# Decode attention with a gated FFN: K and V in pairs of heads, wo as the last load

## The chip, the cores and the metric

The kernel runs on one NeuronCore of a Trainium2 chip. The metric is device time in microseconds (us), the median of several executions. Times come from runs in the fast state. A profile shows one execution: its "span" is 1.5 to 1.8 us shorter than the measured time of the same execution, so spans are compared with spans.

## The reference

Two sequences, one query token each, 32 heads of 128, a cache of 4096 keys. In short:

```python
q = (x @ wq) per head                      # wq 512 x 4096
p = softmax(q k^T / sqrt(128))             # k_cache, v_cache: 2 x 32 x 4096 x 128, bf16
a = concat_heads(p v) @ wo                 # wo 4096 x 512
b = relu(x @ w1) @ w2                      # FFN, 1376 wide
g = sigmoid(sum(x * gate_w))
out = g * a + (1 - g) * b
```

K and V are 134 MB of the 145.4 MB that must come from HBM. Everything else is small.

## The kernel before

One load is one head of K or V, 1 MB, one row of 8 KB in each of 128 partitions, into one of 8 slots. All K heads come first, then all V heads. w1 and w2 are loaded after the sixth K head, wo in the middle of K.

```python
    for n in range(128):
        s = n % NSLOT                                   # NSLOT = 8
        waits = []
        if n >= NSLOT:
            prev = n - NSLOT
            waits.append(f"T_{prev}_3" if prev < 64 else f"pv_{prev - 64}")
        P.add("sp", lambda e, n=n, s=s: e.dma_start(kv_sb[:, s, :], kv_in(n)), ...)
        # [...] w1, w2 at n == 5, wo at n == 40
```

So a K slot is free when its transposes are done, a V slot when its product with p (PV) is done. For each K head TensorE (PE) makes 32 transposes (T) into PSUM; VectorE (DVE) and ScalarE (ACT) copy them to SBUF; then 8 score matmuls (Sc) follow. Each goes to one of four column groups of the array, given by `tile_position`. PE runs one head ahead: T of head i+1 stands before Sc of head i.

```python
    def S_chunk(g, c):
        p0 = 32 * (c % 4)                               # column group
        return bank(2 * g + c // 4, 0, 512, p0, p0 + 32)
    # [...]
    for g in range(2):                                  # batch
        P.begin_loop(NIT)
        for p in range(PER):
            T((p + 1) % PER, lambda t, g=g, p=p: 32 * g + PER * t + p + 1)
            Sc(g, p)                                    # c = 0..7, 512 columns each
        P.end_loop()
    # [...]
    ptrans(0)                                           # p of batch 0 to PV's layout
    denom(0)
    # [...] PV of batch 0
    ptrans(1)
    denom(1)
    # [...]
    ffn_h()                                             # FFN, between the two halves of V
    ffn_f()
    # [...] PV of batch 1, projection of each head after it
```

Of the kernel before, what the change touches and what calls it, by code (L numbers as in the profile page):

```python
# [13 lines left out]
NSLOT = 8  # L14
PER = 8
NIT = 32 // PER
# [3 lines left out]
class _Op:  # L20
    __slots__ = ("fn", "waits", "signal", "sem")

    def __init__(self, fn, waits, signal, sem):
        self.fn = fn
        self.waits = waits
        self.signal = signal
        self.sem = sem

# [8 lines left out]
class _Prog:  # L37
# [19 lines left out]
    def add(self, engine, fn, waits=(), signal=None, sem=None):  # L57
        op = _Op(fn, waits, signal, sem or engine + "_ev")
        if engine == "pe" and self.loop is not None:
            self.loop.ops.append(op)  # L60
        else:
            self.streams[engine].append(op)
# [8 lines left out]
    def _count(self, op, name, counts, inc):  # L71
        if name is None:
            return
        counts[op.sem] = counts.get(op.sem, 0) + inc
        assert name not in self.marks, name
        self.marks[name] = (op.sem, counts[op.sem])

    def resolve(self):
        counts = {}
        for e in self.ENGINES:  # L80
            for it in self.streams[e]:
                if isinstance(it, _Loop):
                    for t in range(it.n):
                        for op in it.ops:
                            if op.signal is not None:
                                self._count(op, op.signal(t), counts, 1)
                else:
                    self._count(it, it.signal, counts, 16 if e == "sp" else 1)
# [22 lines left out]
    def emit(self, engine, eng):  # L111
        for it in self.streams[engine]:
            if isinstance(it, _Loop):
                lin = [self._linear(op, it.n) for op in it.ops]
                with eng.Fori(0, it.n) as iv:
# [5 lines left out]
                    for op, ws in zip(it.ops, lin):  # L121
# [3 lines left out]
                        if op.signal is not None:  # L125
                            ins.then_inc(self.sem(op.sem), 1)
            else:
# [3 lines left out]
                if it.signal is not None:  # L131
                    ins.then_inc(self.sem(it.sem), 16 if engine == "sp" else 1)


def bass_gated_mix__gqa_block_cached__dense_activation_relu__decode_kernel(
# [17 lines left out]
    jmask = sb("jmask", [128, 32], f32)  # L153
    ones = sb("ones", [128, 128], f32)
# [13 lines left out]
    kv_sb = sb("kv_sb", [128, NSLOT, 4096], b16)  # L168
    kt_sb = sb("kt_sb", [128, NKT, 32, 128], b16)
    qmask = sb("qmask", [128, 64, 32], b16)  # L170
    qst = sb("qst", [128, PER, 32], b16)
    E_sb = [sb(f"E{g}", [128, 1024], b16) for g in range(2)]
    pst = sb("pst", [128, PER, 32], b16)
# [8 lines left out]
    oT = sb("oT", [128, 32, 2], b16)  # L182
# [18 lines left out]
    PT_BANK = (0, 2)  # L201
    MISC = 1
    A_BANK = 3
    HT0 = 0

    def o_col(p):
        return bank(4 + p % 4, p, 1)
# [3 lines left out]
    w1_in = B_w1.rearrange("(t p) f -> p t f", p=128)  # L211
    w2a_in = B_w2[0:1280, :].rearrange("(t p) n -> p t n", p=128)
    w2b_in = B_w2[1280:1376, :]
    wq_in = A_wq.rearrange("(t p) n -> p t n", p=128)
    wo_in = A_wo.rearrange("(h d) n -> d h n", d=128)
    out_ap = out.rearrange("b s d -> (b s) d")

    def kv_in(n):
        c = A_k_cache if n < 64 else A_v_cache
        b, h = divmod(n % 64, 32)  # L220
        return c[b, h].rearrange("(p r) d -> p (r d)", p=128)


    def load(name, dst, src, waits=()):
        P.add("sp", lambda e: e.dma_start(dst, src), waits=waits, signal=name, sem=name)  # L225

    load("ld_x", x_sb[:, :], x_in)
    load("ld_gw", gw_sb[:, :], gw_in)
    load("ld_wq", wq_sb[:, :, :], wq_in)
    for n in range(128):  # L230
        s = n % NSLOT
        waits = []
        if n >= NSLOT:
            prev = n - NSLOT
            waits.append(f"T_{prev}_3" if prev < 64 else f"pv_{prev - 64}")
        P.add("sp", lambda e, n=n, s=s: e.dma_start(kv_sb[:, s, :], kv_in(n)),  # L236
              waits=waits, signal=f"ld_kv_{n}", sem=f"slot{s}")
        if n == 5:
# [3 lines left out]
        if n == 40:  # L242
            load("ld_wo", wo_sb[:, :, :], wo_in)
    P.add("sp", lambda e: e.dma_start(out_ap, out_sb[:, :]), waits=["res"], signal="st", sem="st")
# [14 lines left out]
    P.add("pool", lambda e: e.memset(ones[:], 1.0), signal="c_one")  # L259
    P.add("dve", lambda e: e.memset(zt[:], 0.0), signal="c_zt")  # L260
# [7 lines left out]
    for t in range(4):  # L268
        P.add("pe", lambda e, t=t: e.transpose(bank16(4, 2 * t, 2), x_sb[0:2, t * 128:(t + 1) * 128], ident16[0:2, 0:2]),
              waits=["c_id", "ld_x"] if t == 0 else [], signal="xT" if t == 3 else None)  # L270
    for t in range(4):
        P.add("pe", lambda e, t=t: e.transpose(bank16(5, 2 * t, 1), gw_sb[0:1, t * 128:(t + 1) * 128], ident16[0:1, 0:1]),
# [25 lines left out]
    def evac_eng(p, q):  # L298
        return "act" if q == 3 or (q == 1 and p % 2) else "dve"

    def T(p, head, only=None):

        for q in range(4):
            for rr in range(8):
                r = 8 * q + rr

                def waits(t, q=q):
                    i = head(t)
                    return ([f"ld_kv_{i}"] if q == 0 else []) + ([f"ev_{i - 1}_{q}"] if i else [f"qm_{g}" for g in range(2)] + ["g"])

                def sig(t, q=q):
                    return f"T_{head(t)}_{q}"

                def fn(e, *_, q=q, rr=rr, r=r):
                    return e.transpose(bank16(4 + q, rr * 128, 128), kv_sb[:, p, r * 128:(r + 1) * 128], ident16[:, :])  # L315
                w = (waits if P.loop else waits(0)) if rr == 0 else []
                s = (sig if P.loop else sig(0)) if rr == 7 else None
                P.add("pe", fn, waits=w, signal=s)

    def Sc(g, p):  # L320
        for c in range(8):
            def fn(e, *_, c=c):
                return e.matmul(S_chunk(g, c), lhsT=qst[:, p, :], rhs=kt_sb[:, p % NKT, 4 * c:4 * c + 4, :],  # L323
                                start=False, stop=True, tile_position=(0, 32 * (c % 4)), skip_group_check=True)

            def waits(t):
                i = 32 * g + PER * t + p
                return [f"qst_{i}"] + [f"ev_{i}_{q}" for q in range(4)]
            P.add("pe", fn, waits=waits if c == 0 else [], signal=(lambda t: f"sc_{32 * g + PER * t + p}") if c == 7 else None)

    def evac(i):
        p = i % PER
        for q in range(4):
            src = bank16(4 + q, 0, 1024).rearrange("p (r c) -> p r c", r=8)
            dst = kt_sb[:, i % NKT, 8 * q:8 * q + 8, :]
            w = [f"T_{i}_{q}"] + ([f"sc_{i - NKT}"] if i >= NKT else [])
            if evac_eng(p, q) == "dve":
                P.add("dve", lambda e, dst=dst, src=src: e.tensor_copy(out=dst, in_=src), waits=w, signal=f"ev_{i}_{q}", sem=f"ev{p}{q}")  # L338
            else:
                P.add("act", lambda e, dst=dst, src=src: e.activation(out=dst, in_=src, func=ACT.Copy), waits=w,  # L340
                      signal=f"ev_{i}_{q}", sem=f"ev{p}{q}")

    def stage_q(i):
        p = i % PER
        P.add("pool", lambda e: e.tensor_copy(out=qst[:, p, :], in_=qmask[:, i, :]),  # L345
              waits=[f"qm_{i // 32}"] + ([f"sc_{i - PER}"] if i >= PER else []), signal=f"qst_{i}", sem=f"qs{p}")

    T(0, lambda t: 0)
    for g in range(2):
        P.begin_loop(NIT)  # L350
        for p in range(PER):
            T((p + 1) % PER, lambda t, g=g, p=p: 32 * g + PER * t + p + 1)
# [4 lines left out]
    def row_max(g):  # L357
        P.add("dve", lambda e: e.tensor_reduce(out=m4[:, g:g + 1], in_=S_region(g), axis=AX.X, op=ALU.max),  # L358
              waits=[f"sc_{32 * g + 31}"], signal=f"m4_{g}")
# [15 lines left out]
    def ptrans(g):  # L375
        for cc in range(4):
            for k in range(8):
                c = cc if k < 4 else cc + 4
                r = 4 * c + k % 4
                col0 = (c // 4) * 512 + (k % 4) * 128  # L380
                pq = 32 * cc
                P.add("pe", lambda e, r=r, pq=pq, col0=col0: e.transpose(  # L382
                    bank16(PT_BANK[g], r * 32, 32), E_sb[g][pq:pq + 32, col0:col0 + 128], ident16[pq:pq + 32, pq:pq + 32],
                    tile_position=(pq, 0)),
                    waits=[] if k else [f"pt_{g}_{cc - 1}" if cc else f"E_{g}"], signal=f"pt_{g}_{cc}" if k == 7 else None)

    def denom(g):
        P.add("dve", lambda e: e.tensor_scalar(out=lm[:, g, :], in0=jmask[:, :], scalar1=l4[:, g:g + 1], scalar2=None, op0=ALU.mult),
              waits=[f"E_{g}", "c_j4"], signal=f"lm_{g}")
        P.add("pe", lambda e: e.matmul(bank(MISC, 32 * g, 32), lhsT=ones[:, :], rhs=lm[:, g, :], start=True, stop=True),  # L390
              waits=[f"lm_{g}", "c_one"] + (["rg_0"] if g else []), signal=f"lb_{g}")
# [5 lines left out]
    def stage_p(i):  # L397
        g, j = divmod(i, 32)
        p = i % PER
        P.add("dve", lambda e: e.tensor_copy(out=pst[:, p, :], in_=PSB[:, 1024 * PT_BANK[g] + j:1024 * PT_BANK[g] + 1024:32]),  # L400
              waits=[f"pt_{g}_3"] + ([f"pv_{i - PER}"] if i >= PER else []), signal=f"pst_{i}", sem=f"ps{p}")

    def o_norm(i):
        g, j = divmod(i, 32)
        p = i % PER
        P.add("dve", lambda e: e.tensor_scalar(out=oT[:, j, g:g + 1], in0=o_col(p), scalar1=rg[:, g, j:j + 1], scalar2=None, op0=ALU.mult),  # L406
              waits=[f"pv_{i}", f"rg_{g}"], signal=f"oT_{i}", sem=f"on{p}")

    def PV(g, p):
        for r in range(32):  # L410
            def waits(t):
                i = 32 * g + PER * t + p
                return [f"ld_kv_{64 + i}", f"pst_{i}"] + ([f"oT_{i - 4}"] if i >= 4 else [])
            P.add("pe", lambda e, iv, r=r: e.matmul(o_col(p), lhsT=kv_sb[:, p, r * 128:(r + 1) * 128], rhs=pst[:, p, r:r + 1],  # L414
                                                    start=(r == 0), stop=(r == 31)),
# [125 lines left out]
```

## Time and profile before

| | before |
|---|---|
| time, median | 356.31 us |
| span of the profile (that execution took 356.67 us) | 354.9 us |
| bytes moved | 145.4 MB, 427 GB/s for most of the span |
| last packet of the loads | 350.0 us |

The page of a profile cuts the span into 40 slices: a digit is an engine's busy share in tenths, PEclk is the granted TensorE clock, GB/s what the DMA engines moved. The chain of waits is followed back from the last instruction to what released each step. The lines are shown in the prediction. The main reading: DMA bounds the whole, PE bounds nothing but is full during K.

### The profile page before, as it was taken

To read this page: it belongs to the slowest core of one execution; us is meant where nothing else is said; L and a number is where in the kernel's file an instruction comes from. 1 tells how busy PE (TensorE), PEld (TensorE's weight loads), DVE (VectorE), ACT (ScalarE), POOL (GpSimd) and SP (SyncE) were. 2 spreads that over 40 slices of the span, in tenths; PEclk is the share of its full clock that TensorE was granted. 3 is DMA by queue.
4 is the path that set the end of the run, shared out by engine and by line. 5 is a ranking of instruction groups with operands and counts; after the bars stand their busy time and mean duration, and the time that the engine had idled before them with its cause. 6 is when DMAs were issued, how large, how long until landed. Compare 5 with 4: busy or idle time off the path is not lost.

```text
span 354.9 us, 11090 instructions
## 1 busy us (share of the span) xinstructions
PE 259.1 (73%) x4951; PEld 201.4 (57%) x4951; DVE 134.3 (38%) x323; ACT 100.3 (28%) x105; POOL 16.6 (5%) x77
## 2 busy tenths in 40 slices
PE   2498499999999844999999773344345995665655
PEld 1386387777877733778777573334344563443432
DVE  1056266766666831666676521111100221111101
ACT  1036066556566561556655300000000000000000
POOL 3010000000000000000000000000000000000000
PEclk9999699999999995999999955555555565555555
DMA  7999999999999999999999999999999999999992
GB/s 278 428 423 386 410 424 428 425 428 427 428 427 429 404 352 424 428 428 428 428 428 428 425 420 425 428 428 427 428 428 428 427 422 428 428 425 428 427 426 90
DMA packets 25036, 145.68 MB, mean 411 GB/s; under 512 B 2133, under 2 KB 7610, under 8 KB 8122
## 3 DMA queue, kind: packets, MB, share of 16 engines
q1 hardware_dynamic: 25018, 145.44, 98.6%
q8 instruction: 12, 0.20, 0.2%
q14 instruction: 6, 0.05, 0.0%
HBM read 145.43 MB, written 0.00 MB: 410 GB/s over the span
## 4 chain that ended last, share of the span: by engine, by line
DMA 52%; PE 38%; SPq 8%; issue 1%; DVE 0%
DMA kv_sb<-in_A_v_cache_dram 41%; PE PS L315 28%; DMA kv_sb<-in_A_k_cache_dram 11%; PE PS L323 8%; SPq L225 8%; PE PS L414 2%; SPq L236 1%; PE PS L421 0%; DVE out_sb L490 0%; PE PS L382 0%
## 5 line engine op out<-in xcount | busy, mean ns | idle before, releaser
L315 PEld LDWEIGHTS PS<-ident,kv_sb 128*128 128x128 bf16 x2080 | 121.9, 100 | 44.5 <-issue 32.9
L315 PE MATMUL PS<-ident,kv_sb 128*128 128x128 bf16 x2080 | 132.9, 224 | 17.1 <-DMA kv_sb<-in_A_k_cache_dram 15.5
L338 DVE COPY kt_sb<-PS 128x1024 bf16<-128x1024 bf16 x160 | 104.9, 687 | 70.6 <-PE PS L315 70.5
L340 ACT ACTIVATE kt_sb<-PS 128x1024 bf16<-128x1024 bf16 x96 | 94.9, 1022 | 94.9 <-PE PS L315 94.9
L414 PE MATMUL PS<-pst,kv_sb 128*128 128x1 bf16 x2048 | 62.8, 165 | 62.4 <-DMA kv_sb<-in_A_v_cache_dram 60.5
L414 PEld LDWEIGHTS PS<-pst,kv_sb 128*128 128x128 bf16 x2048 | 59.2, 104 | 77.5 <-issue 70.9
L406 DVE TENSOR_SCALAR oT<-PS,rg 128x1 bf16<-128x1 f32 x64 | 14.1, 221 | 125.4 <-PE PS L414 125.4
L323 PE MATMUL PS<-kt_sb,qst 128*32 128x512 bf16 x512 | 39.8, 388 | 0.0
L433 ACT ACTIVATE hr_sb<-PS 128x20 f32<-128x20 f32 x1 | 0.2, 188 | 73.8 <-PE PS L429 73.8
L345 POOL COPY qst<-qmask 128x32 bf16<-128x32 bf16 x64 | 13.1, 211 | 161.7 <-PE PS L323 148.7
L421 PE MATMUL PS<-wo_sb,oT 128*2 x32 | 18.4, 574 | 0.0
L323 PEld LDWEIGHTS PS<-kt_sb,qst 128*32 128x32 bf16 x512 | 7.7, 94 | 6.7 <-issue 0.2
L288 PE MATMUL PS<-xT_sb,wq_sb 128*128 128x2 bf16 x128 | 3.6, 165 | 9.5 <-DMA wq_sb<-in_A_wq_dram 9.5
L400 DVE COPY pst<-PS 128x32 bf16<-128x32 bf16 x64 | 10.4, 180 | 0.0
L288 PEld LDWEIGHTS PS<-xT_sb,wq_sb 128*128 128x128 bf16 x128 | 3.5, 104 | 9.6 <-DMA wq_sb<-in_A_wq_dram 9.6
L444 PE MATMUL PS<-w_sb,hT_sb 128*2 128x512 bf16 (+1 forms) x11 | 4.9, 630 | 0.6 <-DVE hT_sb L436 0.6
L293 DVE TENSOR_SCALAR qmask<-PS 128x32 bf16<-128x32 f32 x2 | 0.4, 311 | 12.7 <-PE PS L288 12.7
L421 PEld LDWEIGHTS PS<-wo_sb,oT 128*2 x32 | 2.5, 79 | 2.4 <-issue 1.9
L371 ACT ACTIVATE E<-PS,negM 128x1024 bf16<-128x1024 f32 x2 | 2.2, 1114 | 4.7 <-DVE negM L366 4.7
L358 DVE TENSOR_REDUCE m<-PS 128x1 f32<-128x1024 f32 x2 | 2.4, 1219 | 2.8 <-PE PS L323 2.8
L382 PE MATMUL PS<-ident,E 32*128 32x32 bf16 x64 | 3.0, 179 | 0.4
L444 PEld LDWEIGHTS PS<-w_sb,hT_sb 128*2 128x2 bf16 (+1 forms) x11 | 1.2, 120 | 3.4 <-issue 2.7
(40 smaller groups left out, 24.6 us busy)
## 6 DMA issues: line engine op xcount, KB each, us to landing
kv_sb<-in_A_k_cache_dram SPq DMA_DIRECT2D x64, 1024.0 KB, 16.0
kv_sb<-in_A_v_cache_dram SPq DMA_DIRECT2D x64, 1024.0 KB, 18.5
wq_sb<-in_A_wq_dram SPq DMA_DIRECT2D x1, 4096.0 KB, 12.5
wo_sb<-in_A_wo_dram SPq DMA_DIRECT2D x1, 4096.0 KB, 27.8
w_sb<-in_B_w_dram SPq DMA_DIRECT2D x1, 1376.0 KB, 28.6
w_sb<-in_B_w_dram SPq DMA_DIRECT2D x1, 1280.0 KB, 30.9
w_sb<-in_B_w_dram SPq DMA_DIRECT2D x1, 96.0 KB, 22.3
x_sb<-in_A_x_dram SPq DMA_DIRECT2D x1, 2.0 KB
```

Of the source, the lines that this page charges most:

```text
L225: P.add("sp", lambda e: e.dma_start(dst, src), waits=waits, signal=name, sem=name)
L288: P.add("pe", lambda e, h=h, t=t: e.matmul(bank(7, 2 * h, 2), lhsT=wq_sb[:, t, h * 128:(h + 1) * 128], rhs=xT_sb[:, t, :], start=(t == 0), ...
L315: return e.transpose(bank16(4 + q, rr * 128, 128), kv_sb[:, p, r * 128:(r + 1) * 128], ident16[:, :])
L323: return e.matmul(S_chunk(g, c), lhsT=qst[:, p, :], rhs=kt_sb[:, p % NKT, 4 * c:4 * c + 4, :], start=False, stop=True, tile_position=(0, 3 ...
L338: P.add("dve", lambda e, dst=dst, src=src: e.tensor_copy(out=dst, in_=src), waits=w, signal=f"ev_{i}_{q}", sem=f"ev{p}{q}")
L340: P.add("act", lambda e, dst=dst, src=src: e.activation(out=dst, in_=src, func=ACT.Copy), waits=w, signal=f"ev_{i}_{q}", sem=f"ev{p}{q}")
L345: P.add("pool", lambda e: e.tensor_copy(out=qst[:, p, :], in_=qmask[:, i, :]), waits=[f"qm_{i // 32}"] + ([f"sc_{i - PER}"] if i >= PER el ...
L400: P.add("dve", lambda e: e.tensor_copy(out=pst[:, p, :], in_=PSB[:, 1024 * PT_BANK[g] + j:1024 * PT_BANK[g] + 1024:32]), waits=[f"pt_{g}_3 ...
L406: P.add("dve", lambda e: e.tensor_scalar(out=oT[:, j, g:g + 1], in0=o_col(p), scalar1=rg[:, g, j:j + 1], scalar2=None, op0=ALU.mult), wait ...
L414: P.add("pe", lambda e, iv, r=r: e.matmul(o_col(p), lhsT=kv_sb[:, p, r * 128:(r + 1) * 128], rhs=pst[:, p, r:r + 1], start=(r == 0), stop= ...
L421: return e.matmul(bank(A_BANK, 0, 512, 0, 2), lhsT=oT[:, bass.ds(h, 1), :], rhs=wo_sb[:, bass.ds(h, 1), :], start=False, stop=True, skip_g ...
L444: P.add("pe", lambda e, ft=ft, n=n: e.matmul(bank(A_BANK, 0, 512, 0, 2), lhsT=hT_sb[0:n, ft, :], rhs=w2_sb[0:n, ft, :], start=(ft == 0), s ...
```

## The change

Its intent is fewer, longer DMA packets (16 KB rows), and a shorter end: wo arrives last, in pieces, and each piece is projected as it lands, so that attention's last steps are hidden behind wo. Heads come in pairs, 2 MB each, into 4 slots; head h of the pair lies in partitions 64h to 64h+63. PE no longer runs ahead; the scores of the two heads stand next to each other; FFN stands between K and V. The core of the diff:

```diff
-NSLOT = 8
-PER = 8
+NSLOT = 4
+PER = 4
+NPAIR = 16
[...]
     def kv_in(n):
-        c = A_k_cache if n < 64 else A_v_cache
-        b, h = divmod(n % 64, 32)
-        return c[b, h].rearrange("(p r) d -> p (r d)", p=128)
+        c = A_k_cache if n < 32 else A_v_cache
+        b, hp = divmod(n % 32, 16)
+        return c[b, 2 * hp:2 * hp + 2].rearrange("h (p r) d -> (h p) r d", p=64)
[...]
-        if n == 40:
-            load("ld_wo", wo_sb[:, :, :], wo_in)
+    WO_CUTS = (0, 16, 24, 28, 30, 32)
+    for k in range(5):
+        lo, hi = WO_CUTS[k], WO_CUTS[k + 1]
+        load(f"ld_wo_{k}", wo_sb[:, lo:hi, :], wo_in[:, lo:hi, :])
[...]
     def Sc(g, p):
         for c in range(8):
+            for hh in range(2):
[...]
+                P.add("pe", lambda e, iv, c=c, hh=hh: e.matmul(
+                    S_chunk(g, c), lhsT=qst[:, p, hh, :], rhs=kt_sb[:, p % NKT, 8 * c:8 * c + 8, 64 * hh:64 * hh + 64],
[...]
-    T(0, lambda t: 0)
     for g in range(2):
         P.begin_loop(NIT)
         for p in range(PER):
-            T((p + 1) % PER, lambda t, g=g, p=p: 32 * g + PER * t + p + 1)
+            T(g, p)
             Sc(g, p)
[...]
     ptrans(0)
     denom(0)
+    ffn_h()
+    ffn_relu()
+    ffn_f()
+    denom_l(1)
+    ptrans(1)
+    denom(1)
[...] PV of all pairs, then the projection, 64 matmuls of 256 columns
```

## The prediction

> **What bounds the kernel now.** First I read the page's slices and queue lines:
>
> ```profile
> PE   2498499999999844999999773344345995665655
> PEclk9999699999999995999999955555555565555555
> GB/s 278 428 423 386 410 424 428 425 428 427 428 427 429 404 352 424 428 428 428 428 428 428 425 420 425 428 428 427 428 428 428 427 422 428 428 425 428 427 426 90
> DMA packets 25036, 145.68 MB, mean 411 GB/s; under 512 B 2133, under 2 KB 7610, under 8 KB 8122
> ```
>
> A slice is 354.9/40 = 8.87 us. Transfers run at 427 GB/s from the second slice to the last but one, so 145.4 MB need 340.6 us; the other 14 us are the start, two dips (slices 3 to 5: w1/w2; 14 and 15: wo) and the end. DMA bounds the whole. The chain of waits says how far off the next bound is. The whole, by engine:
>
> ```profile
> DMA 52%; PE 38%; SPq 8%; issue 1%; DVE 0%
> ```
>
> The piece (start us, length us):
>
> ```profile
> 102.52 0.55 PE PS L323 x8
> 103.07 1.89 PE PS L315 x32
> 104.96 0.55 PE PS L323 x8
> 105.51 1.89 PE PS L315 x32
> ```
>
> During K the chain runs through PE. A head costs 32 transposes, 1.89 us, and 8 score matmuls, 0.55 us: 2.44 us. Its 1.049 MB cost 2.46 us at 427 GB/s. So PE and DMA are balanced to 1%, and PE has nothing to give away. The stretches confirm it: columns are busy us (instructions) of PE, PEld, DVE, ACT, POOL, then clock, DMA share, GB/s.
>
> ```profile
> 36.00:110.00 74.00, 69.49 (x1118) 55.02 (x1120) 45.83 (x70) 40.54 (x42) 5.71 (x27) 0.95 1.01 426
> 204.00:350.00 146.00, 84.21 (x2110) 64.14 (x2106) 20.22 (x124) 0.24 (x2) 0.00 (x0) 0.51 1.00 420
> ```
>
> K: PE full and DMA full. V: DMA full, PE half busy at half clock. Last, one head's scores, asked of the timeline twice, with a window that touches only the first four matmuls and one that touches all eight:
>
> ```profile
> 61.00 0.40 PE L323 MATMUL PS<-kt_sb,qst 128*32 128x512 bf16 x4
> ...
> 61.00 0.62 PE L323 MATMUL PS<-kt_sb,qst 128*32 128x512 bf16 x8
> ```
>
> Four end together after 0.40 us, eight after 0.62: two rounds 0.22 us apart. In the trace's start times the first four lie 3 ns apart, the next four begin 217 ns later, and the next transpose 0.55 us after the first. Chunks c=0..3 go to four column groups (32*(c%4)) and run side by side; c=4..7 wait for their groups.
>
> **What the Trainium skill says.** "TensorE: Matmul & The Clock Gate", Part 3, The mechanism: matmuls start and end in program order, with no reordering, though different tiles of the array overlap. The trace agrees as far as it shows (3 ns inside a round, 217 ns between rounds), but it has no matmul that follows another in the same group. Same page, Part 1: the array runs at half rate until a free-running window of 3.4 us was busy. Here the first transposes come 107 ns apart from 18.1 to 23.3 us, then 56; after the last scores the clock falls at 204.2 us, 5.45 us later. "DMA: Bandwidth & Descriptors", Why small descriptors are slow: a fixed cost per packet. The trace agrees: packets take 309 ns (8192 B), 109 (2752 B), about 48 (1024 B), which fits 8 ns plus bytes/27.2 per ns.
>
> **The change, part by part.**
>
> *Packets.* Rows of 16 KB, if they stay one packet, take 8 + 602 = 610 ns instead of 2 x 309. A pair (128 rows, 16 engines) takes 4.88 us; all of K and V save 64 x 0.064 = 4 us. wo took 4096 x 48/16 = 12.3 us, now 9.8; w1/w2 took 7.6, now 6.6. DMA's need falls by 7.5 us to about 339. This is the intended gain.
>
> *K on PE, the part that decides.* Sixteen score matmuls per pair, the same 512 in all, but in the order c0h0, c0h1, c1h0, c1h1: two heads of a chunk follow each other in one column group. c0h1 must wait for c0h0's 217 ns; c1h0 starts with c0h1; c1h1 waits again. Rounds: c0h0 | c0h1,c1h0 | c1h1,c2h0 | ... | c7h1, nine, instead of four. So 9 x 0.217 + 0.11 (drain: 0.55 - 2 x 0.217) = 2.06 us where two heads took 1.10. Transposes: 64 at 55.7 ns + 0.11 = 3.67 us. Also the eighth group of transposes waits for ACT's second copy (ACT does copies 1, 3, 5 at 1.02 us each; PE gets there at 3.12 us, ACT at about 3.24): 0.1. A pair is 5.8 us, against 4.88 for its DMA. PE becomes the bound of K. The later score waits (copies 4 to 7) are hidden by the slower scores.
>
> K starts when q is there. wq is now issued first on its queue, 0.7 us earlier: transposes from 17.4 us instead of 18.1. They are cold about 5.2 us, which loses 2.4. K ends at E = 17.4 + 2.4 + 32 x 5.8 = 205.4, say 205.5; before it ended at 198.75. PE does not wait for data: pair n starts at 19.8 + 5.8n, its data lands at about 17 + 4.9n (+6.6 after n=12). With four slots DMA is ahead and idles from pair 20 or so.
>
> *From K to V.* Before, DMA lagged behind PE: at 198.75 us 81.8 MB had moved, 3.6 of them V, four to five more heads lay queued, and the first PV (203.2) freed a slot before they ran out. Now DMA has nothing left: V0 to V3 fill the four slots, the last issued when pair 31's transposes end (E-2.06), landed at about E+4. V4 waits for the first PV, and all softmax and now also all FFN stand before it:
>
> ```profile
> 198.88 1.22 DVE L358 TENSOR_REDUCE m<-PS 128x1 f32<-128x1024 f32 x1 [2.75 <-PE PS L323]
> ...
> 201.61 1.11 ACT L371 ACTIVATE E<-PS,negM 128x1024 bf16<-128x1024 f32 x1 [4.68 <-DVE negM L366]
> ...
> 277.21 4.85 PE L444 MATMUL PS<-w_sb,hT_sb 128*2 128x512 bf16 x11 [0.61 <-DVE hT_sb L436]
> ```
>
> Maximum done E+2.8, exponentials E+4.1; rg_0 E+3.5 (reciprocal 0.36, scale 0.24); 44 FFN matmuls at 27 ns, E+4.8; relu and scaling, E+5.8; FFN's second layer 22 of 256 columns, cold half of the 427 ns start to start seen here, 4.7 us, E+10.5; transposes of p, 64 at 27 ns, E+12.2; denominator E+12.9; its reciprocal and staging E+13.9; PV of 64 at 26.5 ns and its signal E+15.8; V4's first packet 1.1 us after its issue (first wq packet 2.51 after issue at 1.42): about E+17, or E+14.5 if the clock is still warm. I take E+16: 12 us of idle DMA.
>
> *V and wo.* 28 pairs x 4.88 + wo 9.8 = 146.4 us of DMA. Data end D = 205.5 + 16 + 146.4 = 367.9; before 350.0.
>
> *The tail.* Before: last V landed 350.35, PV 1.0, projection 1.1, copy 0.68, store; span ends at 354.9, 4.9 us after the last packet. Now PV and spreading of o hide under wo. But 64 projection matmuls of 256 columns start only when half of wo is there, at D-4.5, and PE is cold: 213 ns each. If the clock rises about 5 us later (24 done), the other 40 take 109 ns: 9.5 us in all, done at D+5. Then copy about 0.4, store and end as before 1.9: D+7.3. The tail grows by about 2.4, though it was meant to shrink.
>
> Sum: 367.9 + 7.3 = 375 span, plus 1.4 (356.3 measured less 354.9 span) = 376.6. I say 376.
>
> **Rivals.** (a) The array runs c1h0 before c0h1, or the two heads side by side. Then scores take four rounds, but the pair still waits for the last PSUM copy: transposes end 3.67, DVE copies 6 and 7 at 0.69 each end near 4.85, scores 0.25 more: 5.15. E = 185, first PV E+16, DMA idle about 8 us: D near 348, end 355, reported 356. For it: different groups do overlap. Against it: the two heads of a chunk use the same group, and order is kept by the page. (b) DMA bound all through, as intended: D = 340.4, plus 3 us of gap at K to V even with PE keeping up, plus 7.3: 351 to 353 reported. Against it: PE was full in K with the cheaper order. Hence over 2% faster (below 349.2) is hardly reachable. (c) Worse: weight loads for a second matmul of the same group aren't hidden, rounds of 0.28 us, pair 6.3, E 16 us later, 390. Against it: FFN's eleven same-tile matmuls come at 427 ns start to start, 512 columns at half clock with nothing added.
>
> **Range and chances.** Nine rounds I hold for about 80% likely; then K gives 370 to 382, its spread from the gap (E+13 to E+18), the clock in the projection (3 us) and 0.1 us per pair (3 us). The rest lies at 351 to 360. The 2% limit, 363.4, is crossed when a pair takes over about 5.4 us. Range 360 to 386; faster 0.04, same 0.18, slower 0.78.
>
> **What would show it.** In the changed profile: a pair's chain of 3.7 us L326 and 2.1 us L337, with L337's sixteen matmuls spread over about 2 us; PE full from 18 to 205 us and GB/s near 360 in the later part of K; GB/s near zero for a slice about 10 us after K; then 430 for V; projection matmuls L482 running past the last data packet by 4 to 5 us. I am wrong if L337 x16 takes near 1.1 us, if GB/s stays at 427 through K, or if V4 is issued without a gap.

## The result, and the profile after

The changed kernel is slower: 366.9 us median of 4 runs (366.51 to 367.09), against 356.36 us in the same rounds. The ratio is 1.027, interval 1.0203 to 1.0338. A ratio here is the mean time of one kernel's fast runs over that of the other's in the same rounds; one run of before took 360.0, so this is a little less than the ratio of the medians, 1.030.

The page of the changed kernel, the same rows as before:

```profile
PE   2499999997999999999997844433344443333457
PEclk9999999999999999999996655555555555555558
GB/s 345 406 427 427 431 429 425 429 417 417 428 427 425 422 429 431 427 427 429 427 425 208 52 429 431 429 431 426 429 427 425 427 426 431 431 429 427 431 405 15
DMA packets 10505, 145.64 MB, mean 399 GB/s; under 512 B 1173, under 2 KB 1274, under 8 KB 1658
```

The dips of before (slices 3 to 5 and 14 to 15) are nearly gone (417 GB/s in slices 9 and 10, counted from 1), and 58% of the packets are gone. In their place is one hole, slices 22 and 23, where K ends and V begins. Stretches of the trace measure it (columns as in the prediction: stretch, length, busy us of PE, PEld, DVE, ACT, POOL, then clock, DMA share, GB/s):

```profile
24.00:190.00 166.00, 162.59 (x2482) 128.20 (x2480) 106.77 (x166) 91.00 (x96) 6.62 (x28) 1.00 1.01 426
...
197.00:208.00 11.00, 9.67 (x194) 7.54 (x195) 3.08 (x16) 0.00 (x0) 0.00 (x0) 0.66 0.01 3
208.00:352.00 144.00, 56.37 (x1950) 54.36 (x1947) 15.49 (x87) 0.00 (x0) 0.00 (x0) 0.50 1.01 426
```

DMA is full all through K, moves next to nothing in these 11 us, and is full again. The chain in order of time, in the middle of K, gives PE's pace:

```profile
131.24 1.54 PE PS L337 x16
132.78 3.68 PE PS L326 x64
136.46 1.54 PE PS L337 x16
138.00 3.68 PE PS L326 x64
```

A pair takes 5.22 us: 3.68 for transposes and 1.54 for scores. Two lines of the timeline say what is in the 1.54 (PEld is the weight load; the bracket is its idle time and the releaser):

```profile
141.60 0.56 PEld L337 LDWEIGHTS PS<-kt_sb,qst 128*32 128x32 bf16 x14
142.61 0.11 PEld L337 LDWEIGHTS PS<-kt_sb,qst 128*32 128x32 bf16 x2 [0.45 <-DVE kt_sb L353]
```

The weights of fourteen of the sixteen scores are loaded within 0.56 us; the last two wait for DVE's last copy out of PSUM. In the trace's start times the first four matmuls come 7 ns apart, the next four begin at 0.227 us, the fourteenth at 0.67 us, and the last two at 1.00 and 1.23 us.

K's scores end at 190.2 us. What stands in the hole is on PE's timeline:

```profile
193.75 2.79 PE L442 MATMUL PS<-xT_sb,w_sb 128*128 128x2 bf16 x44 [1.39 <-DVE rg L406]
197.15 4.68 PE L460 MATMUL PS<-w_sb,hT_sb 128*2 128x256 bf16 x22 [0.61 <-DVE hT_sb L451]
201.76 1.89 PE L394 MATMUL PS<-ident,E 32*64 32x32 bf16 x64
...
205.17 1.97 PE L433 MATMUL PS<-pst,kv_sb 128*128 128x2 bf16 x68 [1.17 <-DVE pst L415]
```

FFN, the second transposes of p, then the first PV, whose end lets V4 be issued at 207.07. V3's last packet had ended at 197.7; DMA then stood still until V4's first packet at 208.0. And the end, as a piece of the chain:

```profile
328.28 1.86 PE PS L433 x64
330.14 0.02 issue
...
330.53 22.10 DMA wo_sb<-in_A_wo_dram
352.63 0.14 issue
352.76 9.97 PE PS L482 x64
```

The projection starts when wo's first 2 MB are in and takes 10 us; the last packet lands at 357.2, so PE runs on for 5.5 us after it.

A balance shows where the time went. At 428 GB/s the 145.4 MB need 339.8 us. Time lost by DMA against that rate, worked out for both traces from the packets of the loads, those at a border in part:

| stretch (us) | before: lost | after: lost |
|---|---|---|
| 0 to 20 | 3.3 | 2.6 |
| 20 to 196 | 4.0 | 1.1 |
| 196 to 210 | 0.2 | 12.6 |
| 210 to the last packet | 2.6 | 1.1 |
| last packet | 350.0 | 357.2 |
| from there to the span's end | 4.9 | 7.8 |

The change won 5.1 us of DMA time outside the hole. The hole cost 12.4 and the end 2.9: together 10.2, the difference of the spans (365.0 less 354.9) to 0.1 us.

### The profile page after: what moved, and what is told of

It reads as the page before. It is cut to its first block, busy times and chain, and to the rows that moved or that the text cites. A ratio compares the mean times of both kernels' runs of the same rounds, so it can differ in the third digit from the quotient of the medians.

```text
span 365.0 us, 10862 instructions
## 1 busy us (share of the span) xinstructions
PE 256.1 (70%) x5028; PEld 211.3 (58%) x5028; DVE 134.1 (37%) x293; ACT 97.2 (27%) x106; POOL 12.0 (3%) x52
## 4 chain that ended last, share of the span: by engine, by line
PE 51%; DMA 44%; DVE 2%; issue 1%; SPq 0%; ACT 0%; DVEq 0%
PE PS L326 29%; DMA kv_sb<-in_A_v_cache_dram 28%; PE PS L337 11%; DMA kv_sb<-in_A_k_cache_dram 10%; DMA wo_sb<-in_A_wo_dram 6%; PE PS L433 5%; PE PS L482 3%; PE PS L460 1%; PE PS L442 1%; DVE m L369 1%; DVE kt_sb L353 1%; PE PS L394 0%; DVE mq L372 0%; DVE negM L377 0%; DVE rinv L405 0%
## 5 line engine op out<-in xcount | busy, mean ns | idle before, releaser
L326 PEld LDWEIGHTS PS<-ident,kv_sb 128*128 128x128 bf16 x2048 | 115.7, 98 | 18.5 <-issue 12.3
L326 PE MATMUL PS<-ident,kv_sb 128*128 128x128 bf16 x2048 | 121.4, 221 | 4.7 <-DMA kv_sb<-in_A_k_cache_dram 3.7
L433 PE MATMUL PS<-pst,kv_sb 128*128 128x2 bf16 x2048 | 59.0, 166 | 86.7 <-DMA kv_sb<-in_A_v_cache_dram 83.1
L422 DVE TENSOR_TENSOR oT<-PS,rg 128x2 bf16<-128x2 f32 x32 | 5.1, 160 | 127.4 <-PE PS L433 127.4
L337 PE MATMUL PS<-kt_sb,qst 128*32 128x512 bf16 x512 | 51.5, 383 | 0.0
L337 PEld LDWEIGHTS PS<-kt_sb,qst 128*32 128x32 bf16 x512 | 17.9, 95 | 21.1 <-DVE kt_sb L353 14.4
L415 DVE COPY pst<-PS 64x64 bf16<-64x64 bf16 x64 | 14.3, 224 | 0.8 <-issue 0.2
L357 POOL COPY qst<-qmask 128x64 bf16<-128x64 bf16 x32 | 7.4, 236 | 156.2 <-PE PS L337 145.3
L482 PE MATMUL PS<-wo_sb,os_sb 128*2 128x256 bf16 x64 | 10.0, 333 | 2.1 <-DMA wo_sb<-in_A_wo_dram 2.1
L482 PEld LDWEIGHTS PS<-wo_sb,os_sb 128*2 128x2 bf16 x64 | 6.5, 102 | 5.4 <-issue 2.2
L519 DVE CAST out_sb<-PS 2x256 bf16<-2x256 f32 x1 | 0.4, 412 | 11.7 <-PE PS L482 11.7
## 6 DMA issues: line engine op xcount, KB each, us to landing
kv_sb<-in_A_k_cache_dram SPq DMA_DIRECT2D x32, 2048.0 KB, 14.6
w_sb<-in_B_w_dram SPq DMA_DIRECT2D x1, 1376.0 KB, 15.8
```

The source lines that it names most:

```text
L326: P.add("pe", lambda e, iv, q=q, rr=rr, r=r: e.transpose(bank16(4 + q % 4, rr * 128, 128), kv_sb[:, p, r, :], ident16[:, :]), waits=waits ...
L337: P.add("pe", lambda e, iv, c=c, hh=hh: e.matmul(S_chunk(g, c), lhsT=qst[:, p, hh, :], rhs=kt_sb[:, p % NKT, 8 * c:8 * c + 8, 64 * hh:64 * ...
L357: P.add("pool", lambda e: e.tensor_copy(out=qst[:, p, :, :], in_=qmask[:, 2 * i:2 * i + 2, :]), waits=[f"qm_{i // NPAIR}"] + ([f"sc_{i - P ...
L415: P.add("dve", lambda e, hh=hh, base=base: e.tensor_copy(out=pst[64 * hh:64 * hh + 64, p, :, hh].rearrange("p (b k) -> p b k", b=2), in_=b ...
L433: P.add("pe", lambda e, iv, r=r, k=32 * b + blk: e.matmul(o_col(p), lhsT=kv_sb[:, p, r, :], rhs=pst[:, p, k, :], start=(r == 0), stop=(r = ...
L482: P.add("pe", lambda e, r=r, a=a: e.matmul(bank(A_BANKS[a], 0, 256, 0, 2), lhsT=os_sb[:, r, :], rhs=wo_sb[:, r, 256 * a:256 * a + 256], st ...
```

## The experiments

All edits are to the changed kernel unless said otherwise, and are shown shortened. "Correct" after a time means that the output agreed with the reference. Pairs are counted from 0, K and V each from 0 to 31. Each run is compared with runs of the kernel before on the same chip (356.25 to 356.29 us median in every batch).

### Four scores in a row in one column group

```diff
-        for c in range(8):
+        for c in (0, 4, 1, 5, 2, 6, 3, 7):
             for hh in range(2):
```

> The changed kernel with its sixteen score matmuls of a pair in the order c0h0, c0h1, c4h0, c4h1, c1h0, ...: four in a row in one column group, the next four in the next. If column groups are independent (a waiting matmul lets later ones of other groups pass), the last matmul still starts when the last PSUM copy is in, about 1.0 us after the first, a pair stays at 5.2 us, and the time at 366.9 within 1 us. If starts keep program order, as my prediction assumed, the sixteen need thirteen rounds of 0.217, a pair takes 6.6 us, K ends 43 us later: about 410 us.

Measured 366.68 us (365.67 to 368.24), correct. The chain of this run:

```profile
131.38 1.54 PE PS L337 x16
132.92 3.68 PE PS L326 x64
136.60 1.54 PE PS L337 x16
```

The pair stays at 5.22 us. In program order, thirteen rounds of 0.217 us would have shown as 2.8 us. So a matmul that waits for its column group does not hold up later ones of other groups. The records do not say which matmul is which, so this rests mainly on the time: matmuls of one group that stay 217 ns apart and keep program order could not finish these sixteen in 1.54. The start times fit. A second matmul starts 14 ns after the first, though the next three in program order share the first one's group. Two more with the longer duration of a group's first (390 ns, not 379) start at 0.34 and 0.41 us, each 0.06 us after the end of a copy for which PE has to wait in this order (ACT's copy 5 and DVE's copy 6).

### PE's old order in K

The second half of a pair's scores is placed after the first half of the next pair's transposes.

```diff
         for p in range(PER):
-            T(g, p)
-            Sc(g, p)
+            T(p, this, 1)                      # second half of this pair
+            Sc(g, p, 0)
+            T((p + 1) % PER, next_one, 0)      # first half of the next
+            Sc(g, p, 1)
```

> The changed kernel with PE's order of before restored: the second half of a pair's scores runs after the first half of the next pair's transposes, so PE does not wait for the last PSUM copies. My theory (K is paced by that wait: 3.68 + 1.54 = 5.22 us a pair against 4.90 for its DMA): a pair falls to 4.9, K ends near 181 instead of 190, DMA still has loads queued then and idles only about 5 us: 357 (355 to 360). Rival (K's pace is not what costs, since the gap hides it): 366.9 within 1.5 us.

Measured 364.96 us (364.25 to 365.39), correct: a miss. Its chain:

```profile
132.54 1.89 PE PS L333 x32
134.44 0.56 PE PS L343 x8
134.99 1.89 PE PS L333 x32
136.88 0.56 PE PS L343 x8
```

The pace is as expected: 2 x (1.89 + 0.56) = 4.90 us a pair. Eight scores that stand as c0h0, c0h1, c1h0, ... take the same 0.56 us as before's eight in four groups, a second sign that the groups are independent. But K ended at 188.9 us, only 1.3 earlier. PE now caught up with the loads and waited for them longer: the issues of pairs 16 and 17, which follow the transposes of pairs 12 and 13, lie 13.5 us apart here and 7.7 in the changed kernel, where w1 and w2 come in between. Later the maximum and exponentials of batch 0 sat in DVE's and ACT's queues in front of copies and cost some microseconds (issues at 115.7, 121.9 and 127.1 instead of 4.9 apart). From there PE needs as long for a pair as DMA, and can't recover. So the faster pace moved K's end by 1.3 us only, and the hole stayed (DMA idle from 197.9 to 206.3). This run can't say what an earlier end of K would be worth.

### FFN in the middle of V

```diff
     ptrans(0)
     denom(0)
-    ffn_h()
-    ffn_relu()
-    ffn_f()
     denom_l(1)
[...]
+    # between pairs 15 and 16 of PV
+    ffn_h(); ffn_relu(); ffn_f()
```

> The changed kernel with all FFN matmuls moved from between K and V to the middle of V. My theory (the idle DMA between K and V is on the path): the first PV comes about 7.7 us earlier, V4 is issued at 199.4 instead of 207.1, idle DMA shrinks from 11 to about 3 us, time 359 (358 to 361). Rival (the gap is covered by queued loads and the loss is elsewhere, in K's pace or the tail): 366.9 within 1 us.

Measured 359.86 us (358.50 to 360.98, 20 runs), ratio 1.008, correct. The stretch of the hole now reads:

```profile
197.00:208.00 11.00, 7.17 (x257) 6.96 (x257) 4.42 (x22) 0.00 (x0) 0.00 (x0) 0.50 0.64 235
```

V4 was issued at 200.3, 6.8 us earlier, DMA idled 3.5 us instead of 10.3, and the last packet came at 351.4. The median fell by 7.0 us, the span of the profiled run by 6.3. The theory holds: what stands between K and V is on the path, nearly microsecond for microsecond.

### Only the first half's work between K and V

FFN as above; also the second transposes of p and the second denominator move to the middle of V, and p of batch 0 is staged before the maximum of batch 1.

```diff
-    row_max(1)
-    exps(1)
     ptrans(0)
     denom(0)
-    [FFN]
-    denom_l(1)
-    ptrans(1)
-    denom(1)
     for i in range(PER):
         stage_p(i)
+    row_max(1)
+    exps(1)
+    denom_l(1)
     [PV of pairs 0 to 15]
+    ptrans(1)
+    denom(1)
+    [FFN]
```

The second denominator's matmul now also waits for pair 15's last step on DVE, which still reads the PSUM bank that it writes. (A first form without this wait was refused by the check before the chip, says the author; the record has no run of it.)

> The changed kernel with only what V's first half needs left between K and V: p of batch 0 is transposed and staged at once, the maximum and exponentials of batch 1 follow on DVE and ACT, and FFN, the second transposes of p and the second denominator move to the middle of V. K itself, its pace of 5.22 us a pair and its end near 190.2 are untouched. My theory (the loss is only the time from V3's landing, 196.5, to V4's issue): first PV about 3 us after K, V4 issued near 195.3, no idle DMA, last packet 11 us earlier at about 346, time 355.4 (354 to 357). Rival (PE's slower pace in K costs time by itself): still several us of idle DMA before or after K, 359 or more.

Measured 355.20 us (354.38 to 356.23), ratio 0.997, interval 0.9958 to 0.9983, correct. The hole is gone:

```profile
24.00:190.00 166.00, 163.46 (x2501) 128.78 (x2498) 107.94 (x168) 91.47 (x97) 6.66 (x28) 1.00 1.01 426
...
197.00:208.00 11.00, 6.31 (x213) 5.90 (x210) 3.73 (x23) 1.21 (x2) 0.00 (x0) 0.50 0.97 398
```

V4 was issued at 195.9 and the last packet came at 347.0, 10.2 us earlier, with K's pace still 5.22 us a pair. That is also 3.0 us before the last packet of the kernel before, whose end is 2.5 us shorter. So the pace did not cost by itself, and the hole was the loss in front of the tail.

### wo in the hole

wo's five loads are issued after V3 (n == 35) instead of last; nothing else.

> The changed kernel with wo loaded between V3 and V4, where DMA idles 11 us, instead of last. wo needs 9.8 us, so the last packet comes 9.8 us earlier, near 347.4. But now PV, spreading and all 64 projection matmuls (10 us, cold first) stand after it: end 347.4 + 0.4 + 1.9 + 1 + 10 + 2.3 = 363 span, 364.4 reported (363 to 366). If wo's place at the end hid nothing, it would gain the whole 9.8: 357. If the gap is not idle in truth, the last packet stays at 357 and the time rises to 374.

Measured 363.92 us (363.12 to 365.63), correct. The last packet came at 347.8, as expected, but 14.9 us passed from there to the end. So wo as the last load does hide about 7 us of attention's end (14.9 against 7.8); filling the hole, 9.4 us in the last packet, is worth more.

### Keeping the clock up before the projection

Matmuls whose result nobody uses are put between the last PVs, and 12 in front of the projection.

```diff
+    for p in range(PER):
+        PV1(28 + p)
+        keep_warm((0, 8, 8, 3)[p])
[...]
     o_spread()
+    keep_warm(12)
     proj()
```

> The changed kernel with only the unneeded matmuls added before the projection, which still starts at wo's first 2 MB. If the clock is what makes 64 matmuls take 10 us, they take 7.0 and the time is 363.9 (363 to 365). If unneeded matmuls do not raise the clock, 366.9 or, since they stand in the way, up to 369.

Measured 365.7 us (364.9 to 366.08), correct: in the expected direction, but less, and outside the range expected. The chain:

```profile
351.39 2.60 PE PS L447 x12
353.99 7.09 PE PS L493 x64
```

The projection takes 7.1 instead of 10.0 us: all 64 matmuls come 109 ns apart, at a granted clock of 1.0 from 348.8 us on, where the changed kernel's first 28 come 213 ns apart. So the clock is the cause of its length. But the twelve matmuls were still running at 353.9, and wo's first piece had landed at 353.1: about 0.8 us was given back. That piece also landed 0.45 us later than in the changed kernel.

### Both repairs, and a smaller first piece of wo

The kernel with only the first half's work between K and V, with `WO_CUTS = (0, 8, 16, 24, 28, 30, 32)`, and one unneeded matmul instead of twelve before the projection. This run is the e5 of the next section.

> The same with two changes at the end: wo's first piece cut in two, so that projection can start 2.4 us earlier, and 20 unneeded matmuls between the last PVs that keep the array's clock up, so that all 64 projection matmuls take 109 ns. My theory (the tail is a cold PE behind a late first piece): projection ends about 1 us after the last packet instead of 5.5, and the time falls 4.7 below the version without: 350.7 (349 to 352.5), faster than both kernels. Rival (the tail is the store's own latency): 355.4.

Measured 353.04 us (352.03 to 354.01), ratio 0.990, interval 0.9886 to 0.9916, correct: faster than both kernels, though by 1.0% only, and 2.3 us above the expectation, outside its range.

```profile
341.04 5.08 PE PS L493 x32
346.12 0.04 issue
346.16 3.67 PE PS L493 x32
```

Projection begins at 341.0 instead of 342.6, and is done 1.6 us after the last packet. The clock had fallen again (0.5 from 340.6 to 344.0), so its first half still ran partly slow. That cost almost nothing: the second half needs wo's third piece, which landed at 346.11, 0.05 us before it starts. From there 32 matmuls take 3.67 us, and the last packet comes 2.1 us after that piece; this gives the 1.6. The last packet itself came 1.2 us later, at 348.2. What each of the two changes is worth alone, this run does not separate.

### The block in the middle of V, split

> The version of e5_early_warm with its block in the middle of V split: the second transposes of p and the denominator after pair 15, FFN after pair 23. In e5 that block held V's slots for 13 us, and DMA idled about 1 us near 276 us. If that is what put its last packet at 348.2 instead of 347, the packet comes back to about 347.2 and the time to 352 (351 to 353). If the late packet came from other causes (the longer program's own fetches), 353.

Edit: in the kernel above, FFN moves from after pair 15 to after pair 23. Measured 353.8 us (352.87 to 355.69), ratio 0.994, correct. The dip at 276 us is gone and the last packet came at 347.3 in the profiled run, whose span is 0.9 us shorter than e5's (351.3 against 352.2). The median is no better, and the six runs spread over 2.8 us: on the time it is inconclusive. Its trace does show what holds the projection, whose matmuls come 109 ns apart here wherever they do not wait for data:

```profile
340.38 3.79 PE L493 MATMUL PS<-wo_sb,os_sb 128*2 128x256 bf16 x32
345.24 3.65 PE L493 MATMUL PS<-wo_sb,os_sb 128*2 128x256 bf16 x32 [1.07 <-DMA wo_sb<-in_A_wo_dram]
```

With the clock up, the first half is done early, the second waits for wo's third piece (landed at 345.19), and the projection again ends 1.6 us after the last packet. So of e5's missing 2.3 us, 1.2 are the late packet and 0.6 the pieces of wo (1.6 instead of 1 us); the rest stays open.

### Rows of 8 KB again

```diff
-        load(f"ld_kv_{n}", kv_sb[:, n % NSLOT, :, :], kv_in(n), ...)
+        for k in range(2):
+            load(..., kv_sb[:, n % NSLOT, 32 * k:32 * k + 32, :], kv_in(n)[:, 32 * k:32 * k + 32, :], ...)
```

> The changed kernel with each 2 MB transfer of K and V issued as two of 1 MB with rows of 8 KB, as before the change. The prediction had 16 KB packets save 0.06 us a pair (610 ns against 2 x 309). If that holds, V's pace rises from 4.90 to 4.96 us a pair and the time by about 1.8 us (28 pairs after the gap), to 368.7. If the rate is capped elsewhere, V's pace stays at 4.90 and the time within 0.5 us of 366.9.

Measured 369.63 us (368.01 to 371.16), ratio 1.038, correct. In V, from 222 to 330 us, DMA moved 422 GB/s here, 429 in the changed kernel and 427 in the one before:

```profile
222.00:330.00 108.00, 40.34 (x1400) 38.97 (x1397) 11.60 (x66) 0.00 (x0) 0.00 (x0) 0.50 1.01 422
```

At 422 GB/s a pair takes 4.97 us, as the expectation had it; the time is 0.9 us above it. So within this layout the long row is worth 1.6%, but against before only 0.4%: before's 8 KB rows lay back to back in HBM, the halves here lie 16 KB apart, and an 8 KB packet takes 312 ns (median) instead of 309. That the distance is the reason is not shown.

### Contiguous weights in FFN's first layer (wrong result on purpose)

```diff
-    lhsT=w1_sb[:, t, ft:1280:10] if ft < 10 else ...
+    lhsT=w1_sb[:, t, 128 * ft:128 * ft + 128] if ft < 10 else ...
```

> Wrong result on purpose. The changed kernel with the FFN's first-layer weights read as contiguous columns of the same tile instead of every tenth column; nothing else. Its 44 matmuls come 58 ns apart in the changed kernel and 27 in the one before. If the column step is what doubles them, they come 27 ns apart again, all after them on the way to V4 comes 1.4 us earlier, and the time is 365.5. If it is something else (the clock, w1's load), they stay at 58 ns and the time at 366.9.

Measured 366.85 us (364.31 to 368.75); the spread hides an effect of 1.4 us on the time, so on that it is inconclusive. The timeline is clear:

```profile
195.54 1.48 PE L442 MATMUL PS<-xT_sb,w_sb 128*128 128x2 bf16 x44 [1.38 <-DVE rg L406]
```

44 matmuls in 1.48 us instead of 2.79, start to start 25 ns instead of 58; a weight load (PEld) takes 96 ns instead of 162. So the column step is what slows them. V4 was issued 15.9 us after the end of K's scores, 16.9 in the changed kernel.

## Why the prediction was right or wrong

The direction was right, the mechanism partly, the size about twice too large: 376 foretold, 366.9 measured, 1.055 against 1.027.

**The step that failed: "Rounds: c0h0 | c0h1,c1h0 | ... | c7h1, nine, instead of four."** The scores of a pair need four rounds; groups do not wait for each other (1.54 us in the order of the change, 1.54 with four in a row, 0.56 for eight). A pair took 5.22 us, close to the 5.15 of rival (a), because of the last copy, as that rival says: the waits for copies 4 to 7, which the prediction held to be hidden by slower scores, set the length of the scores. From this, E (the end of K's scores) was 190.2 instead of 205.5.

**"PE becomes the bound of K", and DMA "idles from pair 20 or so": wrong.** DMA was full until 197 us. Restoring 4.90 us a pair gained 2 us, and removing the hole with 5.22 kept gained 11.7 (366.9 less 355.2). PE was slower than DMA through most of K, but the queue of four slots absorbed it: a K load took 14.6 us (median) from its issue to landing, about three pairs of DMA work, and V3, the last load before the hole, still took 9.5 us.

**Rival (a) also had the time wrong,** 356 instead of 366.9: it took E for 185, and what follows E for as short as the main forecast did. K starts at 17.9, loses 1.3 to the cold clock, takes 32 x 5.22 = 167.0, and waits 2.5 for the pairs behind w1/w2 and 1.0 around the softmax of batch 0: 189.7, against 190.2 measured. The waits were left out of it.

**The hole: right in kind, its size in part by luck.** "12 us of idle DMA" measured 10.3 between V3's last packet and V4's first. First PV at E+15.0 (said: about E+14), V4's issue at E+16.9 (said: 15.8), its first packet at E+17.8 (taken: 16). FFN's first layer took 2.8 us, said 1.2, for the column step. V3's data ended at E+7.5, not E+4, since DMA still had a queue. The two errors offset each other.

**The tail: right.** "D+5" for the projection, measured D+5.5; from the last packet to the end 7.3 said, 7.8 measured.

**The packets: too large.** 610 ns said, 613 measured (median), but 4 us of gain for K and V did not come: V's pace went from 4.90 to 4.89 us a pair. The term that was wrong is that of before: 2 x 309 ns make 4.94 us a pair, and two heads took 4.90 there. Why is not shown; the DMA share is 1.01 in both traces. "About 339" is the sum of packet times, some 346, less 7.5, and not the 340.6 of its first paragraph less 7.5. The gain at w1/w2 and wo is in the balance above.

**The sum.** E was foretold 15.3 us too late; V4's first packet came 1.8 later after E than said; V and wo took 2.8 longer; the tail 0.5 longer. As spans: 375.2 - 15.3 + 1.8 + 2.8 + 0.5 = 365.0, as measured. The "1.4" from span to time set the median against the span of a slower execution; within one execution it was 1.8 before and 1.5 after.

Chances of 0.78 for slower and a range of 360 to 386 held; the centre did not.

## What to carry to other kernels

Where DMA is the bound, look at the moment at which one stream's buffers must come free for the next: here, whatever stood in front of the first release was paid nearly in full, whatever the engines' load elsewhere. Before charging an engine's slower pace, count what is queued between it and the bound. And put at such a border only the work that the next release needs; the rest has room in the middle of a stream, where this kernel's PE is half idle.

## What the Trainium skill lacked or had wrong

- "TensorE: Matmul & The Clock Gate", Part 3, The mechanism, has matmuls start and end in program order with no reordering. Here sixteen matmuls, four in a row in the same column group, took 1.54 us where order would need 2.8; eight with pairs in one group took 0.56 us, as eight spread over four groups do. Within these runs, column groups waited for themselves alone.
- The same page, Part 4, says that the full clock does not engage for transposes. In the kernel before, PE ran nothing but transposes from 18.1 to 24.2 us, and their distance fell from 107 to 56 ns at 23.3 us, where the granted clock rises to 1.0; in the changed kernel it stays there from 20.6 to 194.7 us of transposes and scores. (The trace names them MATMUL and does not show whether the transpose mode was set.)
- The same page, Weight-path perf modes, gives the range of column steps in which fast weight load works, but no cost inside it. With a step of ten columns the matmuls came 58 ns apart, with contiguous columns 25.
- "DMA: Bandwidth & Descriptors", Measured, has 341 GB/s for 1 MB and 425 for 16 MB, for transfers issued from GpSimd. With several transfers queued from SyncE, 1 MB ones moved 427 GB/s here and 2 MB ones 429: the size of one transfer hardly counted. We found no page with the cost of splitting rows, 422 against 429 GB/s.
